# A fused attention, capacity-routed experts and cosine MLP on one core: raw weights after the first shifts, one-hot matrices of eight columns, the last pairs' rows turned after the scores

## The chip, the cores and the metric

The kernel runs on 1 core of one Trainium2 chip. The metric is the device time of one execution in microseconds; lower is better. Three runs of the kernel before the change took 1143.96, 1136.66 and 1138.93 us, a median of 1138.93 us.

## The reference

Three stages follow each other. `q`, `k`, `v` have 4 batches, 12 heads, 448 rows and 64 columns; there are 1792 tokens of 768 columns, 8 experts with 1024 inner columns, and a last MLP with 2048 inner columns, all in float32.

```
q_n, k_n = rmsnorm(q, g_q), rmsnorm(k, g_k)
attn = softmax(q_n @ k_n^T / 8);  x = (attn @ v) as 1792 rows of 768
logits = x @ w_gate                       # 1792 x 8
for idx in argsort(-logits.flatten()):    # greedy, best score first
    tok, e = idx // 8, idx % 8
    if assigned[tok] >= 0 or counts[e] >= 224: continue
    assigned[tok] = e; counts[e] += 1
x = for each expert e: relu(x[mask_e] @ w1[e]) @ w2[e]
h = x @ w_in;  out = (h * cos(h)) @ w_out
```

The greedy assignment is kept exactly: every expert receives 224 tokens, which expert fills up first decides which is computed next, and the threshold of an expert is found digit by digit in the bits of the scores.

## The kernel before, in words

**Planner.** Two objects of class `Plan` (L52) collect steps, one for the attention and one for the experts and the MLP. `Plan.run` (L182) orders the steps of each plan by a list schedule: it knows a cost for each instruction (`cost`, L66), the dependencies (`touch`, L136, by tile and byte range, or by a string used as a token), a due time worked back from the end, and `rush`, which makes steps more urgent. It then issues all instructions in that order; each engine and the DMA queue of SP work through their own list in order. The second plan's tiles are allocated in a pool that is opened when the pool of the first is closed.

**Attention** (`attention`, L368). Two heads are a pair, and there are 24 pairs (`NPR`). For a pair, `front` (L658) loads q and k and computes the norms, `turn` (L490) transposes them, `shifts` (L515) computes a bound of each row's maximum: seven score matmuls, reduced by VectorE to `cm`, transposed, negated by ScalarE to `cr` and written by two small DMAs on SP's queue to a row of `sr` (`copy`, L423). `scores` (L555) makes the scores transposed, in four blocks of 112 keys; the shift enters as one more matmul (`st<-sr,heads`), and ScalarE takes the exponential. `weigh` (L587) multiplies by v, sums, and multiplies by the gate's weights. `finish` (L678) calls `rows` (L624), which makes the reciprocal sums `r` and the logits, and `pair` (L693), which calls `tail` (L639): four transposes of the pair's result `xe`, then the scaling by `r` into `xk`, on VectorE in two instructions, or on ScalarE in eight for the last `XKL` = 1 pairs. Three pairs fill one `xk`, which is stored to x in HBM.

**Raw weights.** The MLP's matrices are split in 56 pieces into a high and a low part (`Narrow.piece`, L299): one raw load, two ScalarE passes, five VectorE passes and one store. The first `EARLY` = 38 pieces are done beside the attention, the next `GAP` = 4 after the first gather, and the other 14 when the first group of experts reaches the output matmuls (`fresh`, L1289).

**Routing** (`Router`, L748). `start` (L991) handles one batch of tokens within the attention; `quick` (L1003) finds the threshold for the first two experts, and `slow` (L1030) for the others. A step of `quick` is a `count` (L950): for each of 16 columns of tokens it builds two one-hot or staircase matrices of 112 x 128 (`A` and `B` in the tile `ab` or `AB`) from the digits `X` and `W`, and a matmul adds their product to a histogram. For 10 of 16 columns `B` is a Sign on ScalarE, otherwise both are on VectorE; the values are -1/+1 or -0.5/+0.5 times 2, which the factor 2 in `up` and `rp2` takes up. `digits` (L970) reads the threshold's digit off the histogram, and `narrow` (L983) makes the next `X` and `W`. `phase` (L1072) then gives every chosen token its slot, builds 16 one-hot matrices `oh` of 112 x 112 from `rel`, and multiplies by the token numbers to get `idx`, with which `route` (L1215) gathers the rows of x (`xr`).

**Experts and MLP** (`moe`, L1176). Experts are taken in groups of two. Route 0 stands alone between the two plans; each later route lies beside the matmuls of the expert or MLP before it. `expert` (L1325) multiplies by `w1` and `w2`; `mlp` (L1356) multiplies by `w_in`, takes the cosine and multiplies by `w_out`.

## Time and profile before

| | us |
|---|---|
| runs | 1143.96, 1136.66, 1138.93 |
| median | 1138.93 |
| profiled execution, its own time | 1139.73 |
| its span, first to last instruction | 1137.8 |
| TensorE (PE) busy | 1082.1 (95%) |
| VectorE (DVE) busy | 888.2 (78%) |
| ScalarE (ACT) busy | 638.1 (56%) |
| GpSimd (POOL) busy | 255.6 (22%) |

Times in the views are microseconds from the first instruction. PE is TensorE's matmuls, PEld its weight loads, DVE VectorE, ACT ScalarE, POOL GpSimd and SP the engine whose queue (SPq) issues most DMAs. An entry such as `AB<-ia,X` names the tile written and the tiles read. A bracket at the end of a row of the timeline gives the idle time of the engine before that row and what released it. In the view by stretch a row holds start and end, the length, then busy us and (instructions) of PE, PEld, DVE, ACT and POOL, and last the granted clock, the DMA share and GB/s. In a list of waits a row says who waited for whom, us in total, how often and the longest. Helper functions record most operations, so nearly all carry line L47, and tiles tell them apart.

### The profile page before, as it was taken

The page shows a single profiled execution, that of the slowest core. Times are in us where ns is not written, and L with a number is a line of the kernel's source. Part 1 is how long each engine was busy: PE and PEld are TensorE (multiplying, and loading weights), DVE is VectorE, ACT ScalarE, POOL GpSimd, SP SyncE. Part 2 cuts the span into 40 slices and gives each one's busy share as a digit, 9 for nine tenths or more (in the row PEclk, how much of TensorE's full clock was granted, in tenths as well). Part 3 has the DMA queues.
Part 4 walks back from the last instruction along what each step waited for, and adds up shares of the span by engine and source line. Part 5 has one row for each costly group of instructions (what it writes and reads, how often), then busy time and mean ns, then how long its engine had stood idle before and what let it go on. Part 6 is the DMA issues. An engine that isn't in the chain of part 4 may idle for free.

```text
span 1137.8 us, 20923 instructions
## 1 busy us (share of the span) xinstructions
PE 1082.1 (95%) x7268; PEld 879.6 (77%) x7268; DVE 888.2 (78%) x2453; ACT 638.1 (56%) x1562; POOL 255.6 (22%) x367
## 2 busy tenths in 40 slices
PE   7999999999967999998989999999999899999997
PEld 5555555555436898987979988899989689999887
DVE  7988989999999969998978896568889477856300
ACT  4788877865653546655656572237666236646300
POOL 3687787766510000000110000020000002000001
PEclk9999999999976999999989999999999999999999
DMA  8153455455653888689867668738856957666652
GB/s 216 49 149 123 147 171 175 164 160 171 223 209 93 254 226 306 243 236 383 275 182 190 233 212 248 275 131 241 238 207 220 316 198 233 195 215 208 243 185 93
DMA packets 172745, 234.35 MB, mean 206 GB/s; under 512 B 14112, under 2 KB 144608, under 8 KB 168032
## 3 DMA queue, kind: packets, MB, share of 16 engines
q1 hardware_dynamic: 170240, 222.01, 61.5%
q0 software_dynamic: 2400, 11.01, 2.7%
q8 instruction: 57, 0.93, 0.3%
q14 instruction: 48, 0.39, 0.1%
HBM read 196.37 MB, written 36.52 MB: 205 GB/s over the span
## 4 chain that ended last, share of the span: by engine, by line
PE 43%; issue 13%; DVE 7%; DMA 6%; ACT 1%; POOL 1%; POOLq 0%; DVEq 0%; ACTq 0%
PE acc L47 41%; DMA xr<-x,idx 2%; DMA ws<-in_moe_w_dram 2%; DVE wx L47 1%; DMA ws<-in_moe_w_out_dram 1%; DVE AB L47 1%; PE rt L47 1%; DVE oh L47 1%; PE tr L47 1%; DVE na L47 1%; ACT wx L1277 1%; DMA wx<-w_out 0%; POOL xr L1228 0%; DVE sm L47 0%; DVE gh L47 0%
## 5 line engine op out<-in xcount | busy, mean ns | idle before, releaser
L47 PE MATMUL acc<-wx,gh 128*128 128x512 f32 (+1 forms) x896 | 228.7, 343 | 0.0
L47 PE MATMUL acc<-x2h,wx 128*128 128x448 f32 x768 | 223.1, 368 | 0.0
L47 PEld LDWEIGHTS acc<-wx,gh 128*128 128x128 f32 x896 | 157.2, 192 | 21.1 <-issue 3.3
L47 PEld LDWEIGHTS acc<-x2h,wx 128*128 128x128 f32 x768 | 144.5, 188 | 11.3
L47 PE MATMUL acc<-wx,gl 128*128 128x512 f32 (+1 forms) x448 | 151.9, 339 | 0.0
L47 PE MATMUL acc<-x2l,wx 128*128 128x448 f32 x384 | 140.2, 365 | 0.0
L47 PE MATMUL acc<-gh,wx 128*128 128x448 f32 (+1 forms) x768 | 130.3, 326 | 3.0 <-DVE gh L47 1.8
L47 POOL TENSOR_TENSOR pa<-pf,pf 112x448 f32<-112x448 f32 x94 | 113.4, 1226 | 70.9 <-ACT pf L47 70.8
L47 DVE TENSOR_TENSOR wx<-ws,wx 128x1024 fp32r<-128x1024 f32 (+1 forms) x96 | 104.4, 1087 | 29.1 <-ACT wx L1277 25.8
L47 PEld LDWEIGHTS acc<-gh,wx 128*128 128x128 f32 x768 | 116.9, 192 | 10.9 <-DVE gh L47 2.3
L1228 POOL DMA_INDIRECT xr<-x,idx x16 | 20.4, 1275 | 449.2 <-issue 140.1
L47 ACT ACTIVATE pf<-st 112x448 f32<-112x448 f32 x192 | 93.7, 538 | 39.7 <-PE st L47 39.0
L47 DVE TENSOR_REDUCE cm<-s 128x1 f32<-128x448 f32 x168 | 100.2, 617 | 15.8 <-PE s L47 13.4
L1277 ACT ACTIVATE wx<-ws 128x1024 fp32r<-128x1024 f32 (+1 forms) x96 | 90.8, 947 | 34.1 <-PE acc L47 16.7
L47 ACT ACTIVATE r<-r 128x448 f32<-128x448 f32 x128 | 73.9, 578 | 53.9 <-DVE r L47 52.0
L47 DVE SCALAR_TENSOR_TENSOR r<-r,acc 128x448 f32<-128x448 int32 (+1 forms) x128 | 77.7, 617 | 33.0 <-ACT r L47 31.7
L47 PEld LDWEIGHTS acc<-wx,gl 128*128 128x128 f32 x448 | 85.8, 192 | 8.6
L47 PE MATMUL acc<-xe,wx 128*128 128x448 f32 x576 | 91.9, 320 | 0.0
L47 PEld LDWEIGHTS acc<-xe,wx 128*128 128x128 f32 x576 | 86.2, 189 | 4.0
L47 ACT ACTIVATE oh<-oh 128x896 bf16<-128x896 bf16 x48 | 45.6, 949 | 77.5 <-DVE oh L47 77.2
L47 PE MATMUL st<-qq,kk 64*112 64x448 f32 x576 | 87.8, 389 | 0.6 <-ACT pf L47 0.6
L1430 POOL DMA_INDIRECT out_dram<-xo,to x14 | 15.1, 1078 | 322.5 <-ACT xo L1398 321.2
(269 smaller groups left out, 1989.5 us busy)
## 6 DMA issues: line engine op xcount, KB each, us to landing
wx<-w_in SPq DMA_DIRECT2D x64, 768.0 KB
wx<-w_out SPq DMA_DIRECT2D x36, 1024.0 KB
ws<-in_moe_w_dram SPq DMA_DIRECT2D x64, 384.0 KB
ws<-in_moe_w_dram SPq DMA_DIRECT2D x48, 512.0 KB
nr<-in_moe_w_in_dram SPq DMA_DIRECT2D x32, 384.0 KB
w_in<-nr SPq DMA_DIRECT2D x32, 384.0 KB
ws<-in_moe_w_out_dram SPq DMA_DIRECT2D x14, 512.0 KB
w_out<-wx SPq DMA_DIRECT2D x14, 512.0 KB
```

What stands on the lines that cost most here:

```text
L47: self.plan.add([(self.eng, self.plan.cost(self.eng, name, out, r, kw), lambda: f(*args, **kw), self.plan.shares(self.eng, name, out, r, k ...
L1228: P.add([("POOL", 2.1 - 0.9 * h, lambda x=x, h=h: nc.gpsimd.indirect_dma_start(out=x, out_offset=None, in_=x_rows, in_offset=bass.Indirect ...
L1277: P.add([("ACT", 0.093 + n * 0.1067, lambda: nc.scalar.activation(hi, s, AF.Copy)), ("DVE", 0.07 + n * 0.0667, lambda: nc.vector.tensor_co ...
L1430: step = nc.gpsimd.indirect_dma_start(out=out, in_=src, in_offset=None, out_offset=bass.IndirectOffsetOnAxis(ap=at, axis=0)).ins
```

## The change

The order of the work, the number of instructions and one constant each change in four places.

- A token `"open"` is written by the second shift copy of pair 0 and read by the raw loads of the attention's weight pieces, by the load of v for pair 2, and by the two loads of the gate's weights, which also move in the program from ahead of pair 0 to after it. SP's queue therefore has them behind that copy.
- `count` and the one-hot matrices of `phase` are built for eight columns (or the four of a batch) with one VectorE instruction for each of the two matrices. For this `X`, `W`, `X0`, `W0` and `rel2` hold every value twice, in bfloat16, and both inputs are repeated by strides of zero. The Sign passes on ScalarE are gone, the matrices hold 0 and 1, and the factor 2 goes with them.
- The tails of pairs 19 to 22 are held back until pair 23 is finished; a token `"shut"` puts the transposes of pairs 19 to 23 behind the last scores. `XKL` = 5 gives the scaling of these five pairs to ScalarE, and `END` = 45 makes the last pair's rows more urgent.
- `EARLY` is 37 in place of 38, so that piece 37 is done after the first gather and piece 41 in `fresh`.

```
+OPEN = ["open"]
...
-        plan.add([("SP", 0.46, lambda: nc.sync.dma_start(r, src))], [], [r], dma=0.0028125 * n * m, land=LAND)
+        plan.add([("SP", 0.46, lambda: nc.sync.dma_start(r, src))], behind, [r], dma=0.0028125 * n * m, land=LAND)
...
-            self.piece(plan, i, raw(), mag())
+            self.piece(plan, i, raw(), mag(), behind=OPEN)
...
-END = 20.0
+END = 45.0
...
-XKL = 1
+XKL = 1+4
+HELD = 4
...
-        recs = ring("r", 3, [CP, NC, 2])
+        recs = ring("r", 3 + HELD, [CP, NC, 2])
...
-                copy(t[h * D:h * D + 1].rearrange("o (m p) -> o m p", p=128), cr[3 * h:3 * h + 4])
+                copy(t[h * D:h * D + 1].rearrange("o (m p) -> o m p", p=128), cr[3 * h:3 * h + 4],
+                     OPEN * (h > P_))
...
-                load(v, P_, 4, t)
+                load(v, P_, 4, t, OPEN * (P_ == 2))
...
+                if P_ == NPR - 1:
+                    P.touch(P.steps[-1], "shut", True)
...
+            if P_ >= NPR - 1 - HELD:
+                P.touch(P.steps[-1], "shut", False)
...
-            pair(P_, r)
+            held.append((P_, r))
+            if not NPR - 1 - HELD <= P_ < NPR - 1:
+                while held:
+                    pair(*held.pop(0))
...
+    def twice(self, x):
+
+        return x.unsqueeze(2).to_broadcast([*x.shape, 2])
+
+    def match(self, out, row, cols, op):
+
+        c, n = out.shape[1:]
+        sh = [out.shape[0], c, n // 2, 2]
+        self.nc.vector.tensor_tensor(out.rearrange("p c (n k) -> p c n k", k=2),
+                                     row.rearrange("p (n k) -> p n k", k=2).unsqueeze(1).to_broadcast(sh),
+                                     cols.unsqueeze(2).to_broadcast(sh), op=op)
...
-        for c in range(cols):
-            A, B, ib = ab[:, 0, c], ab[:, 1, c, 0:n], P["ib"][0:CP, 128 - n:]
-            if c * SIGNS % 16 < SIGNS:
-                nc.scalar.activation(B, ib, AF.Sign, bias=W[:, c:c + 1], scale=-1.0)
-                nc.either("tensor_scalar", A, P["ia"][0:CP], X[:, c:c + 1], None, op0=ALU.is_equal)
-            else:
-                nc.either("tensor_scalar", B, ib, W[:, c:c + 1], 0.5, op0=ALU.is_le, op1=ALU.subtract)
-                nc.either("tensor_scalar", A, P["ia"][0:CP], X[:, c:c + 1], 2.0, op0=ALU.is_equal, op1=ALU.mult)
-            if not whole:
-                nc.tensor.matmul(p[:, 0:n], A, B, start=(c == 0), stop=(c == cols - 1))
-        if whole:
-            nc.begin()
-            for c in range(cols):
+        step = min(cols, 8)
+        for a in range(0, cols, step):
+            cs = slice(a, a + step)
+            self.match(ab[:, 0, cs], P["ia"][0:CP], X[:, cs], ALU.is_equal)
+            self.match(ab[:, 1, cs, 0:n], P["ib"][0:CP, 128 - n:], W[:, cs], ALU.is_le)
+            if whole:
+                nc.begin()
+            for c in range(a, a + step):
                 nc.tensor.matmul(p[:, 0:n], ab[:, 0, c], ab[:, 1, c, 0:n], start=(c == 0), stop=(c == cols - 1))
-            nc.finish()
+            if whole:
+                nc.finish()
...
-        v.scalar_tensor_tensor(P["X"], F, T, X, op0=ALU.subtract, op1=ALU.add)
-        v.scalar_tensor_tensor(P["W"], F, T, W, op0=ALU.is_equal, op1=ALU.mult)
-        v.tensor_tensor(P["X"], P["X"], P["Z"], op=ALU.min)
+        v.scalar_tensor_tensor(P["XF"], F, T, X, op0=ALU.subtract, op1=ALU.add)
+        v.tensor_tensor(P["X"], self.twice(P["XF"]), self.twice(P["Z"]), op=ALU.min)
+        v.scalar_tensor_tensor(P["W"], self.twice(F), T, self.twice(W), op0=ALU.is_equal, op1=ALU.mult)
...
-        for c in range(NCOL):
-            nc.either("tensor_scalar", oh[:, c], P["io"], rel[:, c:c + 1], None, op0=ALU.is_equal)
+        for a in range(0, NCOL, 8):
+            self.match(oh[:, a:a + 8], P["io"], P["rel2"][:, a:a + 8], ALU.is_equal)
...
-EARLY = 38
+EARLY = 37
```

The planner's cost of a two-source VectorE operation on bfloat16 operands of more than 64 elements is halved as well, so the new instructions enter the schedule with that cost.

## Rows read from the trace of the kernel before

**Rows 1.** Busy time by stretch, in the five engines' order.

```profile
27.00:56.00 29.00, 27.79 (x227) 16.85 (x226) 28.32 (x77) 23.37 (x92) 20.11 (x31) 1.00 0.18 52
...
250.00:322.00 72.00, 67.47 (x609) 37.66 (x607) 67.53 (x166) 44.88 (x99) 42.39 (x38) 1.00 0.62 208
...
330.00:354.00 24.00, 11.94 (x62) 7.67 (x63) 21.16 (x134) 5.68 (x21) 0.00 (x0) 0.50 0.38 125
...
524.60:556.00 31.40, 31.29 (x197) 27.97 (x197) 31.26 (x78) 17.04 (x31) 0.00 (x0) 0.95 0.92 321
```

**Rows 2.** PE's waits, 250 to 322 us: total, times, longest.

```profile
PE t L47 <- DVE xk L47: 0.8, 1, 0.8
...
PE t L47 <- DVE part L47: 0.5, 1, 0.5
```

**Rows 3.** Timeline of the start: start and duration in us first.

```profile
13.67 5.18 SPq L309 DMA_DIRECT2D nr<-in_moe_w_in_dram  x4
...
19.93 1.45 SPq L424 DMA_DIRECT2D sr<-cr  x2
...
25.21 0.64 PE L47 MATMUL st<-sr,heads 64*112 64x448 f32 x2 [1.31 <-DMA sr<-cr]
...
27.09 0.68 DVE L47 SCALAR_TENSOR_TENSOR kk<-t,gcol,kk 128x448 fp32r<-128x448 f32 x1 [1.56 <-ACT kk L47]
```

**Rows 4.** Timeline, tail of pair 21: transposes and product.

```profile
305.61 0.60 PE L47 MATMUL t<-ident,xe 128*112 128x128 f32 x4
...
307.83 0.74 DVE L47 TENSOR_TENSOR xk<-t,r 112x256 f32<-112x256 f32 x2
```

**Rows 5.** Timeline from the last scores to the first AB.

```profile
321.29 0.37 PE L47 MATMUL st<-sr,heads 64*112 64x448 f32 x2
...
324.43 0.63 ACT L47 ACTIVATE nr<-na 128x512 fp32r<-128x512 f32 x1 [1.14 <-issue]
...
327.24 1.73 ACT L47 ACTIVATE xk<-t,r 112x64 f32<-112x64 f32 x8
...
328.99 0.63 SPq L704 DMA_DIRECT2D x<-xk  x1
...
333.60 0.69 ACT L47 ACTIVATE AB<-ib,W 112x128 bf16<-112x128 bf16 x2 [3.44 <-DMA x<-xk]
```

**Rows 6.** SP's own waits, 326 to 352 us.

```profile
SPq L309 <- DMA x<-xk: 2.5, 1, 2.5
```

**Rows 7.** Timeline of VectorE, first expert's routing chain.

```profile
333.55 0.26 DVE L47 TENSOR_SCALAR AB<-ib,W 112x128 bf16<-112x128 bf16 x1
...
337.69 0.16 DVE L47 CAST tot<-rt 128x2 fp32r<-128x2 f32 x1
...
339.67 0.23 DVE L47 SCALAR_TENSOR_TENSOR W<-F,PF,W 112x16 f32<-112x16 f32 x1
...
343.94 0.16 DVE L47 CAST tot<-rt 128x2 fp32r<-128x2 f32 x1
...
351.11 2.46 DVE L47 TENSOR_SCALAR oh<-io,rel 112x112 bf16<-112x112 bf16 x15
```

**Rows 8.** Timeline, two prices; tile na, ns min/median/max.

```profile
425.67 1.22 DVE L47 TENSOR_TENSOR wx<-ws,wx 128x1024 fp32r<-128x1024 f32 x1
...
890.63 0.69 DVE L47 TENSOR_SCALAR oh<-AB,b 128x896 bf16<-128x896 f32 x1 [1.07 <-DMA AB<-rows]
...
L47 DVE SCALAR_TENSOR_TENSOR na<-ws,na x12: 670/674/684, 526.7 to 548.6; 128x512 int32<-128x512 int32 x12
```

**Rows 9.** PE's waits, second, fourth and sixth expert.

```profile
PE tr L47 <- DMA xr<-x,idx: 0.9, 1, 0.9
PE rt L47 <- DVE pv L47: 0.8, 1, 0.8
...
PE tr L47 <- DMA xr<-x,idx: 4.5, 2, 2.5
...
PE tr L47 <- DMA xr<-x,idx: 3.7, 1, 3.7
```

More of the change, by code (lines that the diff above doesn't have):

```diff
@@ L97, in cost @@
             x.space == bass.MemoryType.PSUM for x in r)
+        fast = fast or (name == "tensor_tensor" and n > 64 and all(x.dtype == BF16 for x in [out] + r))
         return 0.068 + n / (1920.0 if fast else 960.0) + small * (0.061 if name == "scalar_tensor_tensor" else 0.03)
@@ L297, in late, with piece @@
         return any(at >= least for (t, x, _), at in self.at.items() if (t, x) == (tag, b))
-    def piece(self, plan, i, raw, mag, parts=None):
+    def piece(self, plan, i, raw, mag, parts=None, behind=()):
         nc, v = self.nc, plan.vector
@@ L414, in zset, with load, copy @@
             P.gpsimd.memset(t.bitcast(F32), val)
-        def load(src, P_, n, t):
+        def load(src, P_, n, t, behind=()):
             b, h0 = P_ // NP, (P_ % NP) * 2
             rows = src[b, h0:h0 + n].rearrange("h (p c) d -> p h (c d)", c=NC)
-            P.add([("SP", 0.46, lambda: nc.sync.dma_start(t, rows))], [], [t], dma=0.32 * n,
+            P.add([("SP", 0.46, lambda: nc.sync.dma_start(t, rows))], behind, [t], dma=0.32 * n,
                   land=LAND if P_ >= 2 else None)
-        def copy(o, i):
-            P.add([("SP", 0.635, lambda: nc.sync.dma_start(o.bitcast(F32), i.bitcast(F32)))], [i], [o],
+        def copy(o, i, signs=()):
+            P.add([("SP", 0.635, lambda: nc.sync.dma_start(o.bitcast(F32), i.bitcast(F32)))], [i], [o, *signs],
                   dma=o.partition_size() * o.free_size() / 89600.0)
@@ L453, in attention @@
         zset(wg, 0.0)
-        for h in range(2):
-            r, c = slice(h * D, (h + 1) * D), slice(2 + 8 * h, 10 + 8 * h)
-            P.add([("SP", 0.46, lambda r=r, c=c, h=h: nc.sync.dma_start(
-                wg[r, :, c], w_gate.rearrange("(e h d) n -> h d e n", h=2, d=D)[h]))], [], [wg[r, :, c]], dma=0.1)
         for t in shift_rows + [heads]:
@@ L654, in tail @@
                     ve.tensor_tensor(o, i, r[:, cs].unsqueeze(3).to_broadcast([CP, 2, 2, D]), op=ALU.mult)
-        roots_of, xk_of = {}, {}
+        roots_of, xk_of, held = {}, {}, []
         def front(P_):
@@ L715, in attention @@
                 values(0)
+                for h in range(2):
+                    r, c = slice(h * D, (h + 1) * D), slice(2 + 8 * h, 10 + 8 * h)
+                    P.add([("SP", 0.46, lambda r=r, c=c, h=h: nc.sync.dma_start(
+                        wg[r, :, c], w_gate.rearrange("(e h d) n -> h d e n", h=2, d=D)[h]))], OPEN, [wg[r, :, c]], dma=0.1)
         P.rush = 0.0
@@ L849, in __init__ @@
         g.memset(t("one", [128, 1]), 1.0)
-        g.memset(t("rp2", [128, 1]), 2.0 * CAP)
         self.first_free()
-        for name in ("m", "mx", "K", "F0", "F1", "Z", "X0", "X1", "X2", "W0", "W1", "W2", "G", "Q", "X", "W", "g"):
+        for name in ("m", "mx", "K", "F0", "F1", "Z", "X1", "X2", "W1", "W2", "G", "Q", "XF", "g"):
             t(name, [CP, NCOL])
+        for name in ("X0", "W0", "X", "W"):
+            t(name, [CP, NCOL, 2], BF16)
         for name in ("t0", "t1"):
@@ L905, in on @@
         t("rel", [CP, NCOL])
+        t("rel2", [CP, NCOL, 2], BF16)
     def flip(self, out, k, tmp):
@@ L939, in parts @@
             v.tensor_scalar(i, K, lo + n, 15, op0=ALU.logical_shift_right, op1=ALU.bitwise_and)
-            v.scalar_tensor_tensor(c[f"X{q}"], c["mx"], -16.0, i, op0=ALU.mult, op1=ALU.add)
+            d = (lambda x: x) if q else self.twice
+            v.scalar_tensor_tensor(c[f"X{q}"], d(c["mx"]), -16.0, d(i), op0=ALU.mult, op1=ALU.add)
             v.tensor_scalar(j, K, lo, (1 << n) - 1, op0=ALU.logical_shift_right, op1=ALU.bitwise_and)
-            v.tensor_scalar(c[f"W{q}"], j, 1.0 - (1 << n), None, op0=ALU.add)
+            v.tensor_scalar(c[f"W{q}"], d(j), 1.0 - (1 << n), None, op0=ALU.add)
         if not rest:
@@ L1109, in phase @@
         v.tensor_scalar(half, rel, CP - 0.5, None, op0=ALU.is_ge)
-        v.scalar_tensor_tensor(rel, half, float(-CP), rel, op0=ALU.mult, op1=ALU.add)
+        v.scalar_tensor_tensor(P["rel2"], self.twice(half), float(-CP), self.twice(rel), op0=ALU.mult, op1=ALU.add)
         v.tensor_tensor(pv[:, :, 1], P["pc"], half.unsqueeze(2).to_broadcast([CP, NCOL, 3]), op=ALU.mult)
```

5 lines of the change are left out of this document (1 added, 4 removed).

## The prediction, as it was put on record

> [...]
>
> **Raw weights behind the first shifts.** The first pair's shifts are written by two copies issued at 19.93 us, behind four raw weight loads on the same queue; the scores that need them start at 25.21, after 1.31 us of idle TensorE, and VectorE idles 1.56 us behind the same transposes [rows 3]. VectorE is then busy 28.3 of 29 us [rows 1], so what it gains is kept. No more than these idle times can be gained: I take -1.3 (bounds 0 and -1.6). What moves on SP's queue is four raw loads, one load of v and two of the gate's weights; all of them now stand behind copies that wait for ScalarE, and the next loads of q and k stand behind them. Their readers come later than this stretch. If that cover were gone, a raw load costs 1.3 (5.18 / 4).
>
> **Last pairs' rows behind the scores.** For pairs 19 to 22, four transposes (0.6 us a pair) and two VectorE products (0.74 us a pair) [rows 4] leave the bound stretch: 4 x 0.53 (the pitch of the transposes without the last one's tail) = 2.1 us of TensorE. The waits on such a product and on the row before it (0.8 and 0.5) [rows 2] go with them. Sum -3.4; bounds -1.5 (VectorE is the limit after all) and -4.5 (all the idle time of that stretch). One raw weight piece fewer and END help VectorE there too; I count nothing for it. The transposes go to the hole, where TensorE is half idle [rows 1]: 0, or at most their 2.4 us if each of them stood in front of the chain.
>
> **What the moved work then holds up.** Here I expect the main loss. The first ScalarE write into AB started at 333.60, 3.44 us idle and released by the store of the last rows of x [rows 5]; the load of raw weights behind that store also waited 2.5 us for it [rows 6], though it touches neither x nor xk. AB belongs to the second plan's pool, and the memory of the first passes to it as a whole: nothing of the second plan may write before the first plan's last store has landed. Before, that cost nothing, for the digits of the chain were ready at the same moment (VectorE wrote its first AB at 333.55 without a gap [rows 7]).
> Now the last five pairs are scaled by ScalarE: 40 instructions at 1.73 / 8 = 0.216 us [rows 5] are 8.65 us, none before the last scores end at 321.66 (S). Before, ScalarE was done at 328.97, S + 7.3, with eight of them; 32 more are 6.9, less 1.1 idle that they can fill and 1.3 for the two passes (0.63 each) of the piece that is gone: S + 11.8. From its end to the write of AB took 4.6 us (328.97 to 333.60). So AB opens at S + 16.4, against S + 11.9 before: +4.5. Bounds: 0 (the tails fit earlier) and +13.9 (the long-gate rival below). I take the value worked out, as ScalarE is otherwise free there. SP's queue holds behind this store the second plan's raw loads, which nobody needs before the first gather.
> END = 45 lets the last pair's chain go ahead of pieces: an nr pass of 0.63 us stood in front of the last xe [rows 5]. The gate hides what that gives, so I count 0; it returns only if the gate does not bind.
>
> **One-hot matrices of eight columns.** No row shows a two-source VectorE operation with only bf16 operands. Bounds for 1024 elements: 1.22 us (wx, two sources in f32), and half of it, 0.61, if two elements go at once, as 0.69 us for 896 elements of one source shows that VectorE can [rows 8]. I take 0.68, pitch 0.62, near that row: its output is bf16 like ours. [...]
> First expert, all on the path. [...] Second count: 339.67 to 343.94 = 4.27; now 0.5 for the digits + 1.94 + 0.45 + 0.25 = 3.15: -1.1. Slot matrices: 15 in 2.46 us, so 2.62 for 16; now 2 x 0.62, less 0.4 for matmuls that follow: -1.0. Sum -2.7 (bounds +1.7, see below, and -3.5). The ten Sign passes on ScalarE go too; they ran beside. The short operations for the factor 2 that go, and XF that comes, are in these 0.5 us or beside others: 0.
> Second expert: its route lies beside TensorE's work. TensorE waits 0.8 us for pv, queued behind the slot matrices, and 0.9 for its gather [rows 9]; with three counts and the slots some 3 us shorter both go: -1.7 (bounds 0 and -1.7). Fourth and sixth expert: TensorE waits 4.5 and 3.7 us for their gathers [rows 9], each behind 16 slot matrices; 2.62 - 1.24 = -1.4 each.
>
> **One piece less in the attention.** The piece numbered 41 is now split inside the first group's last block. On VectorE it is five passes of at most 0.67 us [rows 8], between 2.0 and 3.4 us, where VectorE is already busy 31.26 of 31.40 us. TensorE is as full there, so the piece first delays the fourth expert's route: up to +2.9; part of it falls where that route waits for ScalarE anyway, so I take +1.0 (bounds 0, 2.9).
>
> **Sum.** -1.3 - 3.4 + 4.5 - 2.7 - 1.7 - 1.4 - 1.4 + 1.0 = -6.4 us. The profiled execution took 1139.73 us, 1.9 more than its span: 1133.3. The median of the three runs is 0.8 lower, so 1132.5; I say **1132**.
>
> **Rivals.**
> - *The gate does not bind.* The planner could run all tails early enough. Then +4.5 goes and END's 0.6 counts: 1132.5 - 5.1 = 1127.4. For it: ScalarE idles in the hole. Against: no tail may start before S, and 8.65 us of scaling do not fit into 11.9 minus 4.6 = 7.3, so the store would have to land faster or the digits come later as well.
> - *The long gate, slower than before.* The tails take turns in two PSUM banks also needed by the last pair's sums, which are read until about S + 5.6, when the last scaling starts [rows 5]. If each pair's transposes (about 1.0 us at the lower clock, from 0.6 at the higher [rows 4]) and scaling (1.73) go one after another with two handoffs of 0.2, five take 15.6 us; AB opens at S + 25.8, 13.9 later than before: 1132.5 + 9.4 = 1141.9. From a gate more than 10.9 us later than before the change loses.
> - *The matches run one element at a time*, as wx does, so the change does not do what it says. Pitch 1.14: first count 5.6 (+1.5 where I have -0.6), second 4.7 (+0.4, not -1.1), slots -0.2, second expert -1.0, the two later routes -0.6 each: 6.7 more, 1139.2. For it: the only two-source rows run so.
> - *The planner's new order.* Changed costs let it shuffle every queue; no row prices that. The largest single wait of rows 9, about 4 us, is what one bad or good choice is worth: 1128 to 1136, in both directions.
>
> **How the numbers follow.** The forecast has 0.45 and its own range, 1127 to 1138; no binding gate 0.25; a new order that dominates 0.12; one element at a time 0.10; the long gate 0.08. A difference under 1% (11.4 us) can hardly be told from none, as three runs of one kernel span 7.3. Below 1127.5 lie 0.13 of the second case (a little over half of it), 0.07 of the forecast and 0.05 of the reordering: 0.25 faster. Above 1150 lie 0.03 of reordering and 0.01 of the long gate: 0.04 slower, 0.71 within. The range reaches from the gate-free case with its upper bounds (1122) to the long gate (1142).
>
> **What would show it.** The new trace should have the first scores near 24 us; no xe transposes of pairs 19 to 22 before the last scores; the last store of x issued some 12 us after them, and the first write of AB right behind its landing; matches of about 0.68 us; shorter waits for the fourth and sixth gather. A first AB write that follows its digits at once proves the gate wrong; matches of 1.2 us prove the price wrong; a later gather of the fourth expert means that the piece cost more than I said.

## The result, and the profile after

The changed kernel is **slower**, by 1.1%: 1149.02, 1151.42, 1153.91 and 1151.09 us, median 1151.26, beside 1137.80 for the kernel before in the same comparison; ratio 1.0112 (95% interval 1.0079 to 1.0145), +13.5 us. I had said 1132, between 1122 and 1142, and gave "slower" 0.04. The profiled execution took 1149.02 us (span 1146.6), the lowest of its four, so the traces differ by only 8.8 us of span: part of the loss lies outside what this one pair of traces shows.

Split at three points that both traces have, these 8.8 us are: last scores S at 323.05, before 321.66 (+1.4); from S to the first write of AB +6.3; from there to the first product of the experts -1.0; from there to the end +2.1. The forecast had -4.7, +4.5, -2.7 and -3.5 for these parts.

First the timeline of the start of the changed kernel (start and duration; in brackets the idle time before a row and what released it); it answers to [rows 3].

```profile
19.90 1.45 SPq L427 DMA_DIRECT2D sr<-cr  x2
23.64 0.37 PE L47 MATMUL st<-sr,heads 64*112 64x448 f32 x2
...
36.85 1.23 DVE L47 SCALAR_TENSOR_TENSOR M<-r,full,base 32x8 bf16<-32x8 f32 x1
36.91 1.13 POOL L47 TENSOR_TENSOR pa<-pf,pf 112x448 f32<-112x448 f32 x1
38.24 1.18 DVE L47 TENSOR_SCALAR lim<-slot 128x8 f32<-128x8 f32 x2
38.24 1.15 POOL L47 TENSOR_TENSOR pa<-pf,pf 112x448 f32<-112x448 f32 x1
...
39.52 0.67 DVE L47 SCALAR_TENSOR_TENSOR kk<-t,gcol,kk 128x448 fp32r<-128x448 f32 x1
...
40.77 0.47 PE L47 MATMUL s<-kk,qq 64*128 64x448 f32 x1 [2.27 <-DVE cm L47]
```

The copies are issued as early as before but land sooner: the first scores start at 23.64 instead of 25.21. The gain is gone by 41 us: VectorE is given five small constants ahead of the next pair's `kk` (`M` and the two of `lim` are three of them), and TensorE then stands 2.27 us for the maxima that hang on it. Most of the delay is not the number of these instructions: `M` takes 1.23 us and the pair of `lim` 1.18, where `M` took 0.26 before and the pair takes 0.24 in e12 below. Each of the two ends with the product `pa` that GpSimd runs beside it.

The handover between the two plans, which answers to [rows 5]:

```profile
322.68 0.37 PE L47 MATMUL st<-sr,heads 64*112 64x448 f32 x2
...
328.45 8.30 ACT L47 ACTIVATE xk<-t,r 112x64 f32<-112x64 f32 x40
...
336.78 0.60 SPq L711 DMA_DIRECT2D x<-xk  x1
336.80 0.37 PE L47 MATMUL rt<-tot,up 128*128 128x2 f32 x1 [2.18 <-ACT xk L47]
...
341.26 0.69 DVE L47 TENSOR_TENSOR AB<-ib,W 112x1024 bf16<-112x1024 bf16 x1 [2.44 <-DMA x<-xk]
```

The 40 scalings end at 336.75, the last store goes out behind them, and the first AB write starts when it has landed, 4.5 us later, at S + 18.2. There is a second hold that I had not seen: `rt`, a PSUM tile of the second plan, waits 2.18 us for the same scalings before the digits can go on.

The routing chain of the first expert, against [rows 7]:

```profile
344.86 0.16 DVE L47 CAST tot<-rt 128x2 fp32r<-128x2 f32 x1 [0.61 <-PE rt L47]
...
349.84 0.16 DVE L47 CAST tot<-rt 128x2 fp32r<-128x2 f32 x1 [0.17 <-PE rt L47]
...
356.77 1.16 DVE L47 TENSOR_TENSOR oh<-io,rel 112x896 bf16<-112x896 bf16 x2
357.84 0.21 DVE L47 TENSOR_TENSOR pv<-pc,pv 112x48 bf16<-112x48 bf16 x1
358.10 1.57 PE L47 MATMUL rt<-pv,oh 112*112 112x6 bf16 x16 [5.17 <-DVE pv L47]
359.71 0.17 DVE L47 TENSOR_REDUCE row<-rt 112x2 f32<-112x6 f32 x1 [0.57 <-PE rt L47]
...
366.94 0.95 PE L47 MATMUL tr<-ident,xr 112*128 112x112 f32 x4
...
370.28 0.60 PE L47 MATMUL acc<-xo,ws 128*128 128x224 f32 x2
```

The counts are as short as I had said. The slot matrices are built in 1.16 us instead of 2.46, but the second product `pv` is queued behind them, and TensorE starts on them only then. Before, it worked through this stretch in one block with the warm-up products:

```profile
351.27 2.61 PE L47 MATMUL rt<-pv,oh 112*112 112x6 bf16 x16 [4.24 <-DVE pv L47]
353.74 4.71 PE L1237 MATMUL acc<-oh 112*112 112x224 bf16 x24
...
361.42 0.60 PE L47 MATMUL tr<-ident,xr 112*128 112x112 f32 x4
363.55 4.25 PE L47 MATMUL acc<-xo,ws 128*128 128x224 f32 x16
```

By stretch (columns as in [rows 1]), the first row is the kernel before, in which the clock is at 0.88 while the gather is awaited:

```profile
358.00:361.00 3.00, 1.77 (x19) 1.39 (x17) 2.94 (x22) 2.57 (x7) 0.23 (x1) 0.88 0.60 183
```

and these are the changed kernel:

```profile
330.00:354.00 24.00, 8.62 (x56) 5.84 (x56) 13.60 (x59) 8.74 (x36) 0.00 (x0) 0.54 0.43 145
...
364.00:367.00 3.00, 2.90 (x18) 2.42 (x17) 2.60 (x18) 0.00 (x0) 0.19 (x1) 0.50 0.63 178
367.00:370.00 3.00, 3.00 (x25) 2.77 (x23) 2.97 (x6) 0.40 (x1) 0.51 (x1) 0.58 0.75 216
```

From 330 to 354 us, in the hole between the two plans, VectorE was busy 21.16 of the 24 us before [rows 1] and is now busy 13.60, TensorE 11.94 and now 8.62: the matches save VectorE's time, but the stretch has become one that waits for ScalarE and a store. TensorE's clock is still at 0.50 from 364 to 367 us, when the first rows are transposed: the first four transposes take 0.95 us instead of 0.60, and from them to the product it takes 3.34 us (366.94 to 370.28) instead of 2.13.

TensorE's waits from 390 us to the end (total, times, longest), which answer to [rows 9]:

```profile
PE acc L47 <- DMA wx<-w_out: 5.0, 2, 2.8
PE tr L47 <- DMA xr<-x,idx: 4.1, 3, 2.5
PE acc L47 <- DVE wx L47: 3.6, 5, 1.1
PE acc L47 <- DVE gh L47: 3.2, 3, 1.6
```

Before, the gathers made 9.1 us of these waits, and the other three kinds 2.0. In sum the gathers gave what I said. Three kinds of waits came that the forecast did not have, the largest for loads of the split weights. One of its two stands in the block in which piece 41 is now split:

```profile
537.58 0.80 PE L47 MATMUL acc<-wx,gh 128*128 128x512 f32 x1 [2.84 <-DMA wx<-w_out]
```

A wait of 2.6 to 3.4 us at this place is in all five kernels with `EARLY` = 37 (this one, e4, e7, e8, e9) and over 0.4 us in none of the fifteen with 38. The others no part of the change seemed to touch. That was the open question with which the experiments began: is the loss in the changed stretches, or in every load?

### The profile page after: what moved, and what is told of

It reads as the page before. It is cut to its first block, busy times and chain, and to the rows that moved or that the text cites. A ratio compares the mean times of both kernels' runs of the same rounds, so it can differ in the third digit from the quotient of the medians.

```text
span 1146.6 us, 20642 instructions
## 1 busy us (share of the span) xinstructions
PE 1082.9 (94%) x7268; PEld 880.7 (77%) x7268; DVE 873.7 (76%) x2219; ACT 629.1 (55%) x1535; POOL 250.8 (22%) x366
## 4 chain that ended last, share of the span: by engine, by line
PE 66%; DVE 16%; DMA 10%; issue 4%; ACT 3%; POOL 1%; SPq 0%; POOLq 0%; ACTq 0%; DVEq 0%
PE acc L47 45%; PE st L47 6%; PE po L47 5%; DVE na L47 4%; DMA ws<-in_moe_w_dram 4%; PE s L47 3%; PE t L47 2%; DMA wx<-w_out 2%; PE dn L47 2%; DVE cm L47 2%; DMA xr<-x,idx 1%; DVE r L47 1%; DVE wx L47 1%; PE po L449 1%; PE rt L47 1%
## 5 line engine op out<-in xcount | busy, mean ns | idle before, releaser
L47 PE MATMUL po<-pf,vr 112*64 112x448 f32 x384 | 82.9, 552 | 0.0
```

What stands on the lines that cost most here:

```text
L47: self.plan.add([(self.eng, self.plan.cost(self.eng, name, out, r, kw), lambda: f(*args, **kw), self.plan.shares(self.eng, name, out, r, k ...
```

## The experiments

Each was timed in five rounds beside the kernel before on the same chip (1136.76 us with e1 to e4, 1138.17 with e5 to e8, 1138.42 with e9 to e12, 1138.26 with e13 to e15, 1138.58 with e16 to e18). Ratios are to that, with their 95% interval.

**e1, e2, e3: one part each on the kernel before.** e1 has only the order on SP's queue, e2 only the matches, e3 only the tails.

```
e1: +OPEN = ["open"]          # read by the raw loads, one load of v and the gate's weights
e2: count, digits, narrow, parts and phase as in the change, with the planner's halved cost
e3: -END = 20.0  -XKL = 1     +END = 45.0  +XKL = 1+4  +HELD = 4   # and the token "shut"
```

> The kernel before with the first part alone: raw loads, the v load of pair 2 and the gate's weights behind the first shift copies. The order of the work on TensorE, VectorE, ScalarE and GpSimd is that of before. Theory (the start's gain is real and is kept while the order stays): first scores' shift at 23.6 instead of 25.2, last scores 1.3 to 1.6 us earlier than before, total 1.3 to 1.6 us less than before (about 1136.4). Rival (what is gained at the start is lost again wherever raw pieces come later): last scores within 0.5 us of before, total the same. Rival (the later raw loads themselves are what slowed the attention of the changed kernel): last scores 2 us or more later than before.

> The kernel before with the one-hot matrices of eight columns alone (with the planner's cost for them). Theory (the matches take operations out of the router's constants and the batches, so the planner orders the whole attention anew, and this order is worse on the chip): five small VectorE constants stand ahead of the second pair's column scaling, TensorE then waits over 2 us for cm near 40 us, and the last scores come 3 to 5 us later than before; after them the chain is about 1.9 us shorter (0.5 + 1.1 + 0.1 measured in the changed kernel, and the slots), so the total is 1 to 4 us above before: 1139 to 1142. Rival (the order lost its time to the held tails or to OPEN): last scores within 1 us of before, total 1133 to 1136.

> The kernel before with the held tails alone (HELD 4, XKL 5, END 45). Theory (the gate): last scores about 3 us earlier than before (318 to 319), the last store of x about 14 us after them, the first AB 18 us after them instead of 11.9; total 2 to 4 us above before, 1140 to 1142. Rival (the tails pay and the loss of the changed kernel lies elsewhere): AB within 13 us of the last scores, total 3 us below before.

Measured: e1 1135.01, ratio 0.9990 (0.9962 to 1.0017); e2 1148.14, 1.0101 (1.0064 to 1.0137); e3 1146.56, 1.0079 (1.0050 to 1.0107). In e1 the last scores come 1.9 us sooner than before, about what I said of the start as long as the order behind it stays; its total is not told apart from before. e2 loses about as much as the whole change, against what I expected: its last scores are at 332.70, 11.0 us late, far ahead of the first expert. e3 loses 10, of which the gate (AB at S + 19.9) explains about 8; its last scores, expected 3 us early, are 5.6 late. Its trace begins with late shift copies (first scores at 26.46, before 25.21). In the ten traces without e1's order the first scores start between 24.6 and 26.5 us, in the ten with it between 21.8 and 23.8. So that order brings them some 3 us sooner, and one execution differs from another by up to 2; one trace does not settle how much the tails alone gain.

**e4: the changed kernel with the last rows of x in memory that is not handed over.** `xk` lies in the memory of a tile of the second plan that is used late, and `r` outside the first plan's pool; the order of all instructions is that of the change.

```
-        xks = ring("xk", 2, [CP, NC, 2 * UP * D])
-        recs = ring("r", 3 + HELD, [CP, NC, 2])
+        xks = turns(*(xo[0:CP, 2 * i:2 * i + 2]. ... for i in range(2)))
+        recs = P.ring(kept)("r", 3 + HELD, [CP, NC, 2])
```

> The changed kernel with xk and r in memory that stays allocated after the attention (xk lies where the experts keep xo, which is written later), so that the second plan's pool doesn't take over memory that the last store of x still reads; the order of all instructions is the changed kernel's. Theory (the pool's handover): the first AB no longer waits for the store of x but follows the digits, at 338.9 instead of 341.3; the histogram's rt still waits for ScalarE's last scaling, because PSUM is handed over too; total 2.4 us less than the changed kernel, about 1149. Rival (AB waits for something else that ends at the same time, or what is gained is waited for again before the first gather): total within 0.7 us of the changed kernel.

Measured: 1137.50, ratio 1.0008 (0.9984 to 1.0032), 13.8 us under the changed kernel: far more than a gate of 4 us can give. In its timeline the gate is only half gone:

```profile
336.40 0.37 PE L47 MATMUL rt<-tot,up 128*128 128x2 f32 x1 [2.18 <-ACT xo L47]
...
338.49 0.69 DVE L47 TENSOR_TENSOR AB<-ib,W 112x1024 bf16<-112x1024 bf16 x1
```

The store no longer holds AB, and AB is written 2.8 us sooner. The PSUM tile still waits for ScalarE. The other 11 us came after that, with nothing else changed but where tiles lie: the second plan's tiles had moved. That gave the next theory, which I called the place.

**e5 to e8.** e5 uses the matches only in the second plan, so that the first plan's instructions are exactly those of before; e6 adds e1's order and e4's memory; e7 is the changed kernel again; e8 is the changed kernel without the tails.

```
e5: count2 (the change's count) in the second plan alone, with its own digits Y0, V0
+        self.digits(p, 128, T[0], first)
+        if first:
+            v.tensor_scalar(P["up"], P["up"].bitcast(F32), 1.5, None, op0=ALU.is_ge)
e6: e5 + e1 + e4
e7: no edit
e8: -END = 45.0  -XKL = 1+4  -HELD = 4     +END = 20.0  +XKL = 1  +HELD = 0
```

> The kernel before with the matches of eight columns in the second plan alone: the batches within the attention and all constants stay as before, so that the attention's order is that of before instruction by instruction; the factor 2 is taken out of up after the first digits. Theory (the matches pay, the attention's new order is what lost): last scores as before (within 1.5 us), first AB at S + 11.9 as before, the two later counts of the first expert and its slots 1.8 us shorter, later gathers up to 3 us earlier; total 2 to 4 us below before, about 1134. Rival (the matches themselves slow VectorE or its neighbours): last scores as before and total above 1138.

> The kernel before with the first part (OPEN), the matches in the second plan alone, and xk and r in memory that stays allocated (xk where xo is); no held tails, EARLY 38, attention's order as before on all engines but SP. Theory: 1.7 for the start, 2 to 3 for the matches, and 0 to 1 for the handover, whose gate did not bind here before: total 1131 to 1133, below both kernels. Rival (what is gained before the second expert is waited for again at later gathers and weights): total within 1.5 us of before.

> The changed kernel itself, unaltered, on the chip of its variants. With xk and r kept it was 13.8 us faster, though its first AB came only 2.8 us earlier, with all later instructions in the same order. Theory (the handover costs 3 us at AB and the rest in later waits for weights and gathers that repeat in every execution): 1149 to 1153 again. Rival (the rest is a difference between chips or between executions): 1138 to 1144.

> The changed kernel with HELD 0, XKL 1 and END 20: no tails held, start and matches as in the changed kernel. Theory (the tails gain about 3 us of TensorE in the attention and lose 6.3 us at the handover): last scores 1 to 4 us later than in the changed kernel, first AB at S + 11 to 12 instead of S + 18.2; total 2 to 5 us below the changed kernel. Rival (the tails are what kept the changed kernel's order from being worse still, as the matches alone put the last scores 11 us later): last scores 7 us or more later, total within 1 us of the changed kernel or above it.

Measured: e5 1141.80, ratio 1.0015 (0.9995 to 1.0036); e6 1139.49, 1.0007 (0.9984 to 1.0030); e7 1152.82, 1.0127 (1.0105 to 1.0149); e8 1150.21, 1.0097 (1.0074 to 1.0120). e5 and e6 missed their expectation, although their counts and gates are as short as planned. e7 shows that the loss repeats. e8 came out as expected: the gate is gone (AB at S + 11.3, in e7 S + 18.2), and S comes 4.1 us later than in e7. So in the changed kernel the tails do shorten the attention, the gate takes more than that back, and both together cost 2.6 us; most of the loss lies elsewhere.

What the slow kernels but e3 share is an address, and e5 and e6 are off in the same way. The constants lie ahead of the second plan's tiles; the change adds `XF` (64 bytes in each partition) and drops `rp2` (32), so the targets of all later loads, `ws`, `wx`, `xr`, move from byte 27136 (106 x 256) to 27168. In e5 they start 192 bytes behind a multiple of 256, in e6 32; in e4, by accident, on one.

**e9 and e10: the place by itself, in both directions.** e9 is the changed kernel with `XF` behind the other tiles and 32 unused bytes in its place. e10 is the kernel before with 32 unused bytes among the constants. Neither changes the order or the instructions.

```
e9:  -"G", "Q", "XF", "g"):    +"G", "Q", "g"):    +t("pad", [128, 8])    +t("XF", [CP, NCOL])   # after rel2
e10: +        t("pad", [128, 8])
```

> The changed kernel with one thing moved: the 64 bytes of XF lie behind the second plan's other small tiles, and 32 unused bytes take their place among the constants, so that the second plan's tiles start at byte 27136 of a partition, as before the change, and not at 27168. Every engine's instructions and their order are the changed kernel's. Theory (the change moved every tile that weights are loaded into off a 256-byte boundary, and each load takes longer): the DMA engines' time falls from about 720 us (62.8% of 1150) to about 700, the waits for weights and gathers after 400 us fall, and the total falls by 8 to 12 us against the changed kernel, to 1140 to 1144; last scores and the first AB stay within 2 us. Rival (the 12 us that the kernel with xk and r kept gained are the handover's, through later waits): total within 2 us of the changed kernel, 1150 to 1153.

> The kernel before with 32 unused bytes among the router's constants and nothing else: the attention's and the second plan's tiles start 32 bytes later, where the changed kernel has them. Order of all instructions as before. Theory (place alone): DMA engines' time up from about 700 to about 720 us, total 6 to 11 us above before, 1144 to 1149. Rival (the place matters only together with the change's order, or not at all): total within 2 us of before.

Measured: e9 1145.14, ratio 1.0057 (1.0034 to 1.0081), 6 to 8 us under the changed kernel (6.1 by the medians to its first runs, 8.0 by the ratios to e7); e10 1149.10, 1.0097 (1.0068 to 1.0127): **10.7 us for 32 unused bytes**. e9 fell 1 us short of the range expected, so the change has other losses too. I had also expected its DMA engines' time to fall from about 720 us to 700. It did not: 716 us (62.5% of 1146.1), beside 715 in the first trace of the changed kernel and 722 in e7. In the changed kernel the price of the place is seen in the total alone. TensorE's waits of e10 from 390 us on:

```profile
PE tr L47 <- DMA xr<-x,idx: 10.6, 5, 3.0
PE acc L47 <- DVE gh L47: 5.0, 5, 1.6
```

Before they are 9.1 and 1.8. From 390 us to the end TensorE is busy 727.7 us instead of 726.0 and VectorE 534.4 instead of 532.5; the rest of what e10 loses there is waiting, and the loads take longer. In the part of the page on DMA queues (packets, MB, share of 16 engines' span), before:

```profile
q1 hardware_dynamic: 170240, 222.01, 61.5%
```

and e10:

```profile
q1 hardware_dynamic: 170240, 222.01, 63.3%
```

The same packets and bytes take 724.6 us of the 16 engines (0.633 x 1144.7) instead of 699.7 (0.615 x 1137.8).

**e16, e17, e18: how far.** The kernel before with 32, 128 and 256 unused bytes at the start of the second plan's own pool, so that the constants stay where they were.

```
+        cst.tile([128, 8], F32, name="pad")      # e16; 32 in e17, 64 in e18
```

> The kernel before with 32 unused bytes ahead of the second plan's tiles alone: the attention's tiles and the constants stay in place. Order unchanged. Theory (the tiles that the second plan's loads write are what counts): total 7 to 11 us above before, as with the shift of all tiles (+10.7); last scores as before. Rival (the attention's tiles counted there): total within 3 us of before.

> The same with 128 unused bytes, so that the second plan's tiles start half way between two 256-byte boundaries. Order unchanged. Theory (only a 256-byte boundary is free of the cost; 192 bytes behind one, the kernel with the matches in the second plan had DMA engine time like that of the shifted ones): total 5 to 11 us above before. Rival (a boundary of 64 or 128 bytes is enough): total within 2 us of before.

> The same with 256 unused bytes: the second plan's tiles move as far as they can here but start on a 256-byte boundary again. Order unchanged. Theory: total within 2 us of before. Rival (any move of these tiles costs, or the room taken does): total 4 us or more above before.

Measured: e16 1149.11, ratio 1.0094 (1.0060 to 1.0127); e17 1147.48, 1.0086 (1.0056 to 1.0115); e18 1137.10, 1.0002 (0.9982 to 1.0021). 32 and 128 bytes cost the same, 256 nothing. The queue that carries the loads, from 375 to 1100 us, in e16:

```profile
q1 hardware_dynamic: 122929, 160.03, 72.5%
```

in e17:

```profile
q1 hardware_dynamic: 123888, 160.56, 72.0%
```

and in e18:

```profile
q1 hardware_dynamic: 123340, 162.24, 71.3%
```

Share times 725 us by MB, that is 3.28, 3.25 and 3.19 us per MB. Over all traces read so, eleven with the targets on 256 bytes lie between 3.138 and 3.222, nine with them off between 3.228 and 3.293: the groups do not overlap, but e9 (3.222) and e2 (3.228) nearly meet. Of the three offsets tried, 32 and 128 bytes cost (e16 +0.94%, e17 +0.86%) and 256 do not (e18 +0.02%). By what mechanism is not shown by any row here; the runs moved the tiles that loads write together with those that stores read, so they do not tell these two apart.

**e11, e12: the parts that pay, on 256 bytes.** e11 is e1's order and e5's matches, with the new small tiles behind the others; e12 is e2 with the place mended.

```
e11: e1 + e5, and   -"XF", "Y0", "V0" ahead of the constants' end     +t("XF", ...) +t("Y0", ...) +t("V0", ...)   # after rel2
e12: e2, and        -"G", "Q", "XF", "g"):   +"G", "Q", "g"):   +t("pad", [128, 8])   +t("XF", ...)   # after rel2
```

> The kernel before with OPEN and with the matches of eight columns in the second plan alone, their new small tiles placed behind the second plan's others, so that all tiles that are loaded into stay where they were before; no held tails, EARLY 38, xk not kept. Theory: start -1.7; matches -0.6 up to the first expert's matmuls (1.9 at its gather, 1.3 of it lost to a later rise of the clock) and up to -2 at later gathers: total 2 to 4 us below before, about 1134 to 1136, and 3 to 5 us below the same without the alignment and with xk kept. Rival (the matches were as worthless as the last try showed, place or no place): total within 1 us of before.

> The kernel before with the matches everywhere and nothing else, as in the run of the matches alone, but with XF placed so that all tiles start where they did before. Order as in that run. Theory (two causes there, order and place): the last scores stay 5 to 11 us later than before, because the order of the attention is still the new one, and the DMA engines' time falls by 15 us or more; total 4 to 8 us below the run of the matches alone, about 1141. Rival (the place also made the attention's last scores late): last scores within 2 us of before, total 1134 to 1137.

Measured: e11 **1131.90, ratio 0.9944 (0.9922 to 0.9967)**, 6.5 us faster than before and 19.4 than the change; e12 1142.20, 1.0036 (1.0013 to 1.0058), 6 under e2. In e11 the last scores are at 319.48 and AB at 331.72, and the experts start 2.4 us sooner than before (361.17, before 363.55). The total is 2 us below the range expected.

```profile
357.41 0.95 PE L47 MATMUL tr<-ident,xr 112*128 112x112 f32 x4
...
361.17 0.60 PE L47 MATMUL acc<-xo,ws 128*128 128x224 f32 x2
```

and of the waits from 390 us on

```profile
PE tr L47 <- DMA xr<-x,idx: 4.3, 3, 2.1
PE acc L47 <- DVE gh L47: 1.6, 3, 0.8
```

remain: 4.8 us less for gathers, and none of the three waits that the change brought is above before by more than 0.9. 2.4 and 4.8 make 7.2, against 6.5 in the medians. The agreement is in part luck: e11's trace is its fastest execution, and its span is 12.4 below that of before. In e12 the last scores are still 12.3 us late (333.96), so that loss is not the place. Its DMA engines' time, expected to fall by 15 us or more against e2, fell from 715 to 712. Two rows by stretch and two of the timeline show how the last scores become late:

```profile
40.00:56.00 16.00, 13.96 (x100) 7.21 (x102) 11.49 (x34) 8.15 (x29) 10.32 (x14) 0.79 0.23 57
...
85.00:100.00 15.00, 12.92 (x101) 6.40 (x99) 13.47 (x22) 6.78 (x15) 10.15 (x11) 0.86 0.86 262
...
42.04 0.74 PE L47 MATMUL s<-kk,qq 64*128 64x448 f32 x1 [2.42 <-DVE cm L47]
...
95.43 0.47 PE L47 MATMUL s<-kk,qq 64*128 64x448 f32 x1 [1.56 <-ACT qq L47]
```

TensorE stands 2.42 us for maxima and 1.56 for a norm, and the clock in the 15 or 16 us around is 0.79 and 0.86. From 30 to 112 us it waits 5.3 us in all, 2.9 more than before, where the clock stands at 1.00 throughout. The time lost to the lower clock, (1 - clock) times the length, is 3.4 and 2.1 in these two stretches and 1.3 in the next one (12 us at 0.89): 6.8. Over the whole attention, from the first scores to the last, TensorE is idle 13.6 us instead of 7.5, and these 6.1 with the 6.8 make the 12.9 us that this stretch is longer. Some 8 of these 12 us are regained behind the last scores, in the hole and at the later gathers; the rest is the 0.36% measured.

The order of the attention's instructions is not the whole cause. Ahead of the wait at 42.04 two small VectorE instructions take 1.24 and 1.03 us beside GpSimd's `pa`, as in the changed kernel. The same is seen in e14 (below), which has the attention's order of e11:

```profile
35.31 1.24 DVE L47 SCALAR_TENSOR_TENSOR up<-tmp,em 128x128 fp32r<-128x128 f32 x1
...
39.34 0.47 PE L47 MATMUL s<-kk,qq 64*128 64x448 f32 x1 [2.16 <-DVE cm L47]
```

In e11 this `up` takes 0.29. Nine of the twenty traces (the changed kernel, e2, e4, e6, e7, e8, e9, e12, e14) have two VectorE instructions stretched so, a wait of 2.2 to 2.4 us for `cm` near 40 us and a clock of 0.50 behind it; the other eleven have none of the three there. All seven with the matches within the attention are among the nine, but e6 and e14 have the order of before. So up to 6 us of e12's loss (2.4 of waiting, 3.4 of clock) hang on whether GpSimd's product falls beside these instructions; that an order makes this likely is argued, not shown.

**e13: e3 without the handover of x.** Its place is on 256 bytes too.

```
e3, and e4's two lines for xk and r, and   +t("pad", [128, 8])
```

> The kernel before with the held tails alone (HELD 4, XKL 5, END 45, as in the run of the tails alone), but xk and r in memory that stays allocated, and all second-plan tiles on 256-byte boundaries, so that neither the place nor the memory of the last store of x counts. Order of all instructions as in the run of the tails alone. Theory (the tails themselves gain nothing: their 2.1 us of TensorE come back as waits for cm under another order, and ScalarE's 40 scalings still hold the PSUM until S + 13.7, 6 us later than before): total 1139 to 1143, 1 to 4 us above before and 5 to 8 below the tails alone. Rival (the tails pay once the gate is gone): total 2 us or more below before.

Measured: 1145.27, ratio 1.0059 (1.0028 to 1.0089), 2 above what I expected at most. The first scores are 1.29 us late as in e3, the last 1.41: under this order the tails gain nothing in the attention. Between the two TensorE is busy 286.6 us instead of 288.9, but idle 10.0 instead of 7.5. TensorE's waits in its last 104 us include

```profile
PE s L47 <- DVE cm L47: 3.6, 5, 2.1
```

where before

```profile
PE s L47 <- DVE cm L47: 1.4, 3, 0.7
```

stood: what the transposes leave is taken by waits for VectorE's maxima. The handover costs nearly as much as in the change:

```profile
322.70 0.37 PE L47 MATMUL st<-sr,heads 64*112 64x448 f32 x2
...
338.50 0.37 PE L47 MATMUL rt<-tot,up 128*128 128x2 f32 x1 [3.20 <-ACT xo L47]
...
340.35 0.25 DVE L47 TENSOR_SCALAR AB<-ib,W 112x128 bf16<-112x128 bf16 x1
```

Without the hold on SBUF, AB still opens at S + 17.3, 5.4 later than before: 3.20 us of it are the wait of the PSUM tile for ScalarE.

**e14, e15: what could still be had.** e14 is e11 with the attention's loads and AB on 256 bytes. e15 is e11 with 40 warm-up products that read a constant, so that they need not wait for the slot matrices.

```
e14: +cst.tile([128, 40], ...)   +pool.tile([128, 24], ...)   +t("padc", [128, 8])
e15: -WARM_B = 24   +WARM_B = 40
     -  pw[0:CP, 0:2 * CP], oh[:, 0], oh[:, 0:2]...   reads [oh, idx[t]]
     +  pw[:, 0:256], M[:, 0:128], M                  reads [M]
```

> The best kernel so far (OPEN, matches in the second plan, second plan's tiles where they were) with three unused pads, so that also the attention's tiles of q, k, v and raw weights and the tile AB start on 256-byte boundaries (q, k, v and AB lay 96 and 224 bytes behind one before). Order unchanged. Theory (place counts wherever the DMA queues are full): the attention's DMAs are not its bound, so the last scores stay within 1 us; AB's rows come a little earlier for the later experts: total 0 to 2 us below the best so far. Rival (every load that starts off a boundary counts, the first ones above all): total 3 us or more below.

> The best kernel so far with the idle-time matmuls of the hole reading M instead of the slot matrices, 40 instead of 24, so that 15 of them run ahead of the slots; all other engines' orders unchanged. Theory (with the matches TensorE starts work in the hole 2 us nearer to the gather, its clock rises only after the first transposes, and 1.3 to 1.6 us are lost there): the clock is at its upper level by the first transposes, the time from them to the first expert's matmuls falls from 3.8 to about 2.2 us, total 1 to 1.5 us below the best so far. Rival (the extra matmuls stand in front of the chain's small ones): gather later by 0.5 us or more, total the same or above.

Measured: e14 1131.42, ratio 0.9933 (0.9905 to 0.9960): the same as e11, so q, k and v do not pay for their place. The raw weights were on 256 bytes in both; e10, which moves them off, costs no more than e16, which does not. The last scores of e14's trace are 3.7 us later than e11's, not within the 1 us expected, with the two stretched VectorE instructions shown above. e15 1130.32, 0.9931 (0.9901 to 0.9962), the lowest median, but not told apart from e11. The clock did what I wanted; in e15:

```profile
355.00:358.00 3.00, 2.61 (x19) 1.68 (x16) 2.48 (x20) 0.00 (x0) 0.03 (x1) 0.75 0.57 175
358.00:361.00 3.00, 2.47 (x29) 2.11 (x29) 2.97 (x7) 0.82 (x2) 1.11 (x2) 1.00 0.26 75
```

In e11 the second of these stretches stands at 0.52. The path from the first transposes to the first product shrinks from 3.76 to 2.85 us; I had expected 2.2.

## Why the prediction was wrong, step by step

Two steps failed, and both stand in the sum at nothing: the place of the new tiles, and the new order of the attention.

- **The place.** "The short operations for the factor 2 that go, and XF that comes, are in these 0.5 us or beside others: 0." I counted the time of these operations and not their bytes. `XF` in and `rp2` out moved every load target of the second plan by 32 bytes, and that alone costs 10.7 us on the kernel before (e10) and 6 to 8 in the changed one (e9). No rival held it; the sum went through rows of engines, and this price stands in none of them.
- **The planner's new order.** It was a rival, priced at 4 us either way, and 0 in the sum. With the tiles on 256 bytes the matches everywhere lose 3.8 us (e12), where their terms (-2.7 for the first expert, -4.5 for the later ones) say -7.2: 11 us off. In e12 the last scores came 12.3 us later, of which some 8 came back. The stretched VectorE instructions and the clock behind the wait for them, in no term either, are up to 6 of the 12.3.
- **Start, -1.3:** right by itself (first scores 1.57 sooner, e1's last scores 1.9), lost in the whole by the delay of the second pair's `kk` described above.
- **Tails, -3.4:** borne out in the changed kernel's order, not in that of before. From the first scores to the last, e7 takes 302.5 us and e8, without the tails, 306.2: -3.7. On the order of before, e13 takes 296.6 and the kernel before 296.5, since waits for VectorE's maxima took the place of what the transposes left. My bound of -1.5 had named VectorE as the limit. Each is one trace.
- **Gate, +4.5:** the mechanism was right, the term mis-sized: +6.3 in the trace of the changed kernel, +6.7 in e9. ScalarE ended at S + 13.7 instead of S + 11.8, and the landing took 4.5 (I had 4.6). What I missed is that PSUM is handed over too: with SBUF kept, AB opens only 2.4 (e4) and 2.6 us (e13 against e3) sooner behind S. Tails and gate together cost 2.6 (e7 against e8), where the sum has 1.1.
- **Matches:** 0.69 us for 1024 elements against my 0.68, second count 3.07 us against 3.15: right. My 0.68 was an estimate, from the 0.69 us of 896 elements of one source [rows 8]; in the trace it is 0.60 us from one match to the next (341.26, then two in 1.28), about half of the 1.22 that `wx` takes for as many elements. The first count's share of the -2.7 is -0.6 (4.14 us before, 3.55 forecast); it was worked out with 0.1 us for a matmul at a speed of TensorE's clock that no run shows. What the runs showed in its place is a granted clock of 0.50 from 341 to 345 us, the eight matmuls behind the last match in 1.03 us, and a count of 3.60 us: -0.54. Of the slots' -1.0 only 0.13 came (2.94 against 3.07 us from the first matrix to `row`), for the second `pv` product is queued behind them and TensorE starts only then; the later rise of the clock took back 1.2.
- **Later gathers, -4.5 in all for second, fourth and sixth:** the sum is near (waits for gathers 9.1 to 4.1 us, 4.3 in e11), the parts are not, and that is luck. At the second expert nothing went: the gather's wait stayed at 0.9, and that for `pv` grew from 0.8 to 1.6, as in every kernel with these matches. The fourth gave -1.3. The sixth's 3.7 went whole, but 2.2 us came back as a wait for `w_out` at 904.8, right behind it.
- **Piece 41, +1.0:** mis-sized. The wait of 2.84 us at 537.58 is at its bound of 2.9, and the clock was 0.50 for some us behind it; `EARLY` was not tried alone.
- **The rivals:** none came near as stated. The long gate (1141.9) took part at under half of what it added; the one-element rival fell with the first match, and the gate did bind.

The whole, in medians: +13.5, and 14.7 when run again (e7). Run by themselves the parts are: place +6 to +8 (e9), tails with gate +2.6 (e7 against e8), matches with the new order +3.8 (e12), start -1.8 (e1, not told from none). That is 11 to 13; the rest is left for piece 41 and for what the parts do to each other. The parts come from different kernels and are not additive to the microsecond.

## What to carry to other kernels

Before costing a change in instructions, list what it allocates: a small tile ahead of large ones moves every load target behind it, and here a start off 256 bytes costs 0.9% of the kernel without one instruction changed. When one memory area is handed to the next stage, work that is moved behind the last compute lengthens the handover: here AB opened 6.3 us later behind S, held in SBUF by the last store (4.5 us from the last scaling to AB), and `rt` in PSUM waited 2.18 us for the same scalings. When parts of a change disagree, rebuild it from the parts that keep the order of the rest: the start's order and the matches of the second plan, with their tiles placed behind the others, turned +13.5 into -6.5 us. And a new order is not priced by its engines' busy time: look in its trace for waits that the traces of the old order lack, and for instructions that take several times their usual length (here 1.23 us instead of 0.26).

## What the runs showed of the hardware

- Load targets 32 or 128 bytes off a multiple of 256 cost 0.94% and 0.86% of this kernel, 256 bytes nothing measurable (0.02%); in the second plan, where the queue of the loads is 70.0% busy from 375 to 1100 us in the kernel before. In the attention no price was seen: e10, which moves its tiles too, costs what e16 does (1149.10 and 1149.11 us).
- Small VectorE instructions beside GpSimd's product `pa` (1.13 us) took 1.03 to 1.24 us, where the same ones take 0.24 to 0.33 in other traces: `M` and `lim` in the changed kernel, `up` and `M` in e12, `up` and `b` in e14. Each ended within 0.2 us of the product. Other VectorE instructions beside it kept their length (`kk` in the kernel before, 0.67); what sets the two kinds apart is not shown.
- In all nine traces with a TensorE wait of 2.2 to 2.4 us near 40 us the granted clock fell to 0.50 behind it (from 42 to 44 us in the changed kernel; in e12 0.79 in the mean from 40 to 56 us); in the other eleven it stayed at 1.00 there. In the hole, work that begins before the data arrives brought it to 1.00 (e15) where it was 0.52 (e11).
- Shift copies with four raw loads behind them instead of ahead let the first scores start at 21.8 to 23.8 us (ten traces) instead of 24.6 to 26.5 (ten traces).
